# Scores of each head over its own 64 rows, in banks of their own

## Chip, cores and metric

The kernel runs on one core of a Trainium2 chip. The metric is the device time of one execution in microseconds (us). Three timed runs of the kernel before gave 193.37, 194.30 and 194.61; the median is 194.3.

## What is computed

An attention with a narrow window and block summaries, then a feed-forward with a maximum of two projections. Batch is 4, heads 8, sequence 768, head dimension 64:

```
k_sum = k.reshape(B, H, nb, 32, D).max(axis=3)         # nb = 24 blocks of 32 keys
v_sum = v.reshape(B, H, nb, 32, D).mean(axis=3)
scores_l = scale * q @ k.T      where |i - j| < 16, else -1e9
scores_s = scale * q @ k_sum.T + log(32)
a = softmax(concat(scores_l, scores_s))
x = a @ concat(v, v_sum)                               # heads side by side: 3072 x 512
out = maximum(x @ w1, x @ w2) @ w_out                  # 512 -> 1024 -> 512
```

Inputs and the output are float32; the kernel multiplies in bfloat16 and accumulates in float32.

## The kernel before

Each batch is handled in pairs of heads (`hp`, 4 of them). The two heads of a pair lie on the two halves of the 128 partitions, 64 rows of head dimension each.

- `load_kq` (L270) loads k and q of a pair; `prep` casts them to bfloat16 (L340), turns them on TensorE (PE) with 6 transposes each (L359), and places k in a tile `kx` on VectorE (DVE, L373), where each of 12 tiles has 64 keys and, beside them, the 24 block maxima (L375, L382). ScalarE (ACT) places q in `qx` (L388). `qx` has two copies of the sequence, one for each head: head 0's q stands in rows 0 to 63 of the first, head 1's in rows 64 to 127 of the second, and the other halves are zero (`zero_qx`, L216 and L217, once per buffer). So one matmul over all 128 rows gives the scores of both heads side by side.
- `scores` works on a group (`grp`, 3 per pair) of 4 tiles of 64 queries: 4 matmuls of 128 columns (L414; in the last group one is split into 96 and 32). In batch 0 the window's mask is added by two matmuls of 256 columns from `hide` (L403); in the others DVE multiplies with `mask` afterwards (L435, L441). One exp on ACT (L426) reads the group's whole bank of 512 columns into `pb`.
- `values` multiplies `pb` with the values and means in `vx` (L460, 8 matmuls of 65 columns); DVE divides by the sums (L472, L474); two pairs are turned (L484) into `xt` (L489).
- `load_v` loads v (L281), casts it on GpSimd (POOL) into `vb` (L340), spreads it by DMA into `vx` (L304), makes means on PE (L313), and spreads these too (L327).
- `maxout` per batch and group: 32 matmuls of 256 columns with w2 - w1 (`wd`, L560), relu on ACT (L565), then the output: 8 matmuls with w1 @ w_out (`w1o`, L574) and 16 with w_out (L581), copied by ACT (L340) and stored by the SP queue (L592, L594). `w1o` is made in the kernel from w1, turned (L516), and w_out (L544).

The order of all this on each engine isn't written by hand. Every step is a task with an engine, a cost in us and a priority; `Plan.run` (L97) plays the tasks through with these costs and takes, per engine, the first ready one; the resulting start order is the program's order. Buffers come from rings (`Ring`, `Buf`): a slot counts as free 0.15 us after its last user's planned end. The 8 banks of PSUM are one ring with caps by kind (two for scores, "sc"). The waits in the built program come from the data that instructions touch, not from the plan.

Of the kernel before, what the change touches and what calls it, by code (L numbers as in the profile page):

```python
# [62 lines left out]
class Plan:  # L63
# [8 lines left out]
    def op(self, engine, us, fn, read=(), write=(), change=(), touch=(), behind=(), prio=0.0, label=""):  # L72
        t = Task()
        t.engine, t.us, t.fn, t.label = engine, us, fn, label
        t.prio = (prio, len(self.tasks))
        t.new, t.behind = [*write, *change], behind
        t.deps = {w for b in (*read, *change) for w in b.writers}
        for b in t.new:
            b.writers.append(t)
        for b in (*read, *touch, *t.new):  # L80
            b.users.append(t)
        self.tasks.append(t)
        return t
# [45 lines left out]
def kernel(  # L129
# [31 lines left out]
    def tiles(name, n, shape, dt):  # L161
        return [const.tile(shape, dt, name=f"{name}{i}") for i in range(n)]


    banks = Ring(list(range(8)), {"kq": 2, "sc": 2, "av": 2, "mm": 3})
    bank_tile = psum.tile([128, 8, 512], F32, name="banks")

    def bank(buf, n=512, dt=F32):
        a = bank_tile[:, buf.slot]
        return (a if dt is F32 else a.bitcast(BF16))[:, 0:n]  # L170

    kqf = Ring(tiles("kqf", 6, [128, 2, J * D], F32))
    kqb = Ring(tiles("kqb", 4, [128, J, 2, D], BF16))
    kxr = Ring(tiles("kx", 4, [128, KW], BF16))
    qxr = Ring(tiles("qx", 4, [128, 2, S], BF16))
    pbr = Ring(tiles("pb", 12, [128, 4, 192], BF16))
    vfr = Ring(tiles("vf", 2, [128, 4, NM, D], F32))
    vbr = Ring(tiles("vb", 1, [128, NM, H, VW], BF16))
# [30 lines left out]
    def fixed_parts():  # L209
        def once(ring, i, us, fn, prio):  # L210
            b = Buf(ring)
            b.take(i)
            op("DVE", us, fn, write=[b], prio=prio, label=f"zeros {i}")

        def zero_qx(t):
            nc.vector.memset(t[0:64, 1], 0.0)  # L216
            nc.vector.memset(t[64:128, 0], 0.0)  # L217

        def zero_kx(t):
            sums = t[:, 0:96 * NT].rearrange("p (t c) -> p t c", c=96)  # L220
            nc.vector.memset(sums[:, :, 64 + nb:96], 0.0)

        for i, t in enumerate(kxr.slots):
            once(kxr, i, 0.15, lambda t=t: zero_kx(t), i - 1)
        for i, t in enumerate(qxr.slots):
            once(qxr, i, 0.9, lambda t=t: zero_qx(t), i - 1)
        for i, t in enumerate(pbr.slots):
            once(pbr, i, 0.2, lambda t=t: nc.vector.memset(t[:, :, 64:128], 0.0), i / 3 - 1)

        def keep(m, base, row, pattern):  # L230
            nc.gpsimd.affine_select(out=m, in_=m, compare_op=ALU.is_ge, fill=NEG, base=base,
                                    channel_multiplier=row, pattern=pattern)

        def make_hide():

            nc.gpsimd.memset(hide[:], 0.0)
            for lo, hi, base in ((0, 64, -16), (96, 128, 96 - 48)):
                keep(hide[lo:hi], base + window - 1, 1, [[0, 4], [-1, 64]])  # L240
                keep(hide[lo:hi], window - 1 - base, -1, [[0, 4], [1, 64]])
            keep(hide[64:96], nb - 1, -1, [[0, 4], [0, 64]])
            nc.gpsimd.memset(hide[0:64, 3, 48:64], NEG)
            nc.gpsimd.memset(hide[96:128, 3, 0:48], NEG)

        def make_amean():

            nc.gpsimd.memset(amean[:], 0.0)
            am = amean[:, :, 64:64 + nb]
            nc.gpsimd.memset(am, 1.0 / block)  # L250
            for base, mult, pat in ((0, 1, [[128, NM], [-block, nb]]),
                                    (block - 1, -1, [[-128, NM], [block, nb]])):
                nc.gpsimd.affine_select(out=am, in_=am, compare_op=ALU.is_ge, fill=0.0, base=base,
                                        channel_multiplier=mult, pattern=pat)
            for t in vbr.slots:
                nc.gpsimd.memset(t[:, :, :, D:VW], 1.0)

        op("POOL", 4.0, make_hide, write=[hide_in], prio=-1, label="hide")
        op("POOL", 2.0, make_amean, write=[amean_in], prio=0.2, label="amean")
        op("POOL", 0.4, lambda: nc.gpsimd.tensor_scalar(  # L260
            out=mask[:], in0=hide[:], scalar1=-1.0 / NEG, scalar2=1.0, op0=ALU.mult, op1=ALU.add),
           read=[hide_in], write=[mask_in], prio=100, label="mask")
# [81 lines left out]
    def prep(b, hp, prio, k_on, q_on):  # L344
# [21 lines left out]
        def order(ps):  # L366
            return bank(ps, S, BF16).rearrange("p (j c) -> p c j", j=J)

        def kt():
# [13 lines left out]
            out=kt()[:, :, 64:64 + nb],  # L383
            in_=ks.ap[:].rearrange("p (o n) -> p o n", o=1).to_broadcast([128, NT, nb])),
           read=[ks], write=[kx[b, hp]], prio=prio, label=f"sums k{tag}")
        for a in range(2):
            r = slice(64 * a, 64 * a + 64)
            op("ACT", 0.8, lambda a=a, r=r: nc.scalar.copy(  # L388
                out=qx[b, hp].ap[r, a, :], in_=order(qps)[r]),
               read=[qps], write=[qx[b, hp]], prio=prio, label=f"place q{tag}")  # L390

    def scores(b, hp, grp, prio, mask_on):


        ps, pb, tag = Buf(banks, "sc"), Buf(pbr), f"{b}{hp}{grp}"

        def view():
            return bank(ps).rearrange("p (i a w q) -> p i a w q", i=2, a=2, w=2)

        def mm():  # L400
            if mask_on == "PE":
                for i in range(2):
                    nc.tensor.matmul(  # L403
                        out=view()[:, i], lhsT=identity[:],
                        rhs=(hide[:, 2 * i:2 * i + 2] if grp == NG - 1 else hide[:, 0:2]).rearrange(
                            "p (o w) q -> p o w q", o=1).to_broadcast([128, 2, 2, 64]),
                        start=(i == 0), stop=False)
            for i in range(4):
                t = 4 * grp + i
                w = kx[b, hp].ap[:, 96 * t:96 * t + 128]  # L410
                at, o = 64 * t + 16, view()[:, i // 2, :, i % 2]
                for n0, n1 in ((0, 64),) if t < NT - 1 else ((0, 48), (48, 64)):
                    c = (at + n0) % S
                    nc.tensor.matmul(out=o[:, :, n0:n1], lhsT=w,  # L414
                                     rhs=qx[b, hp].ap[:, :, c:c + n1 - n0],
                                     start=(mask_on != "PE"),
                                     stop=(mask_on != "PE" or (i == 3 and n1 == 64)))

        op("PE", 0.25 + (0.23 if mask_on == "PE" else 0), mm, read=[kx[b, hp], qx[b, hp], hide_in],
           write=[ps], prio=prio, label=f"scores {tag}")  # L420

        def pv():
            a = pb.ap[:, :, 0:128]
            return bass.AP(a.tensor, a.offset, [a.ap[0], a.ap[1], [128, 2], [1, 64]])

        op("ACT", 0.7, lambda: nc.scalar.activation(  # L426
            out=pv(), in_=bank(ps).rearrange("p (i w q) -> p i w q", w=2, q=64),
            func=ACT.Exp, bias=bias[:], scale=scale),
           read=[ps], write=[pb], prio=prio, label=f"exp {tag}")

        def hidden_out():
            eng = nc.vector if mask_on == "DVE" else nc.gpsimd
            if grp < NG - 1:
                m = mask[:, 0:1].rearrange("p w (o q) -> p w o q", o=1).to_broadcast([128, 4, 2, 64])
                eng.tensor_tensor(out=pv(), in0=pv(), in1=m, op=ALU.mult)  # L435
            else:
                o = pv().rearrange("p (i a) w q -> p i a w q", a=2)
                for i in range(2):
                    m = mask[:, 2 * i:2 * i + 2].rearrange("p (o w) q -> p o w q", o=1).to_broadcast(
                        [128, 2, 2, 64])  # L440
                    eng.tensor_tensor(out=o[:, i], in0=o[:, i], in1=m, op=ALU.mult)  # L441

        if mask_on != "PE":
            op(mask_on, 0.43 if grp < NG - 1 else 0.56, hidden_out, read=[mask_in], change=[pb], prio=prio,
               label=f"mask {tag}")
        return pb
# [3 lines left out]
    def values(b, hp, grp, pb, prio):  # L450
# [5 lines left out]
        def mm():  # L456
            for u in range(2):
                for a in range(2):
                    for par in range(2):
                        nc.tensor.matmul(out=av()[:, u, a, :],  # L460
                                         lhsT=pb.ap[:, 2 * u + a, 64 * par:64 * par + 128],
                                         rhs=vx[b].ap[:, 4 * grp + 2 * u + par, 2 * hp + a, 0:D + 1],
                                         start=(par == 0), stop=(par == 1))

# [211 lines left out]
```

## Time and profile before

| | |
|---|---|
| median of three runs | 194.3 us |
| the profiled execution, first to last instruction | 192.5 us |
| PE busy | 166.4 us (86%) |
| ACT busy | 114.1 us (59%) |
| DVE busy | 109.9 us (57%) |
| mean granted PE clock | 0.991 |
| score matmuls (L414) | 208 |
| exps (L426) | 48, 0.686 us each |
| placing q (L388) | 32, 0.791 us each |

The profiled execution has no time beside its span; the timed runs lie 0.9 to 2.1 us above it. Busy times are from one execution. PE's loads of weights (PEld) run beside its matmuls, and a matmul's recorded duration is longer than the distance to the next one, so the distance between starts is the better price of a matmul. A group's line gives: source line, engine, operation, output and input tiles, shapes and count; then busy us and mean ns; then the engine's idle time before, and who ended it. A line of waits gives: who waited for whom, us in total, times, longest.

### The profile page before, as it was taken

How to read it: one execution, taken by the hardware profiler on the slowest of the kernel's cores; microseconds unless marked ns; L12 is line 12 of the kernel's file. 1: busy time of each engine (PE TensorE's matmuls, PEld its weight loads, DVE VectorE, ACT ScalarE, POOL GpSimd, SP SyncE). 2: the span in 40 equal slices, each digit the busy share in tenths (PEclk: the TensorE clock that was granted, in tenths of full speed). 3: DMA queues.
4: the chain of work that ended last, by engine and by line, in shares of the span. 5: the costliest groups of instructions: out<-in, count | busy, mean ns of one | idle time of the engine just before them, and what ended most of it. 6: DMA issues, size and time to landing. Idle time of an engine off the chain costs nothing.

```text
span 192.5 us, 4148 instructions
## 1 busy us (share of the span) xinstructions
PE 166.4 (86%) x1643; PEld 117.9 (61%) x1664; DVE 109.9 (57%) x289; ACT 114.1 (59%) x173; POOL 25.7 (13%) x39
## 2 busy tenths in 40 slices
PE   0629619899999969999979999999999999999990
PEld 0426419865757738758657767487696676665740
DVE  6908956888979438759868953079777600000000
ACT  2533964384689949219967955179986443342621
POOL 7556221300330003300003300000000000000000
PEclk9999996999999999999999999999999999999999
DMA  5999999999999999999999996061020111120303
GB/s 187 226 305 356 234 240 347 371 381 281 210 359 251 292 268 217 339 309 217 229 288 223 340 218 193 3 164 24 3 109 5 54 58 59 50 109 0 112 0 109
DMA packets 47859, 37.27 MB, mean 194 GB/s; under 512 B 26208, under 2 KB 43744, under 8 KB 47840
## 3 DMA queue, kind: packets, MB, share of 16 engines
q1 hardware_dynamic: 47840, 37.01, 71.8%
q8 instruction: 13, 0.21, 0.5%
q14 instruction: 6, 0.05, 0.1%
HBM read 25.17 MB, written 6.29 MB: 163 GB/s over the span
## 4 chain that ended last, share of the span: by engine, by line
PE 53%; DMA 33%; SPq 5%; DVE 4%; POOL 2%; issue 1%; ACT 0%; ACTq 0%
PE banks L581 17%; PE banks L560 16%; DMA vf<-in_v_dram 13%; DMA vx<-vb 10%; PE banks L574 7%; PE banks L460 5%; DMA wf<-in_moe_w_out_dram 4%; SPq L503 4%; DMA vx<-vx 4%; PE banks L414 3%; DMA kqf<-in_k_dram 2%; PE banks L359 2%; POOL vb L340 2%; PE banks L484 2%; PE banks L313 1%; DVE pb L435 1%
## 5 line engine op out<-in xcount | busy, mean ns | idle before, releaser
L560 PE MATMUL banks<-xt,wd 128*128 128x256 bf16 x384 | 46.6, 273 | 0.5 <-DVE xt L489 0.5
L581 PE MATMUL banks<-wo,g 128*128 128x512 bf16 x184 | 44.9, 379 | 0.4
L560 PEld LDWEIGHTS <-wd 128*128 128x128 bf16 x384 | 36.4, 98 | 6.1 <-issue 0.7
L426 ACT ACTIVATE pb<-banks,bias 128x512 bf16<-128x512 f32 x48 | 31.5, 686 | 10.2 <-PE banks L414 9.9
L565 ACT ACTIVATE g<-banks 128x512 bf16<-128x512 f32 x48 | 28.3, 596 | 13.7 <-PE banks L560 13.2
L340 ACT COPY o<-banks 128x512 f32<-128x512 f32 x24 | 14.0, 585 | 28.7 <-PE banks L581 28.4
L388 ACT COPY qx<-banks 64x768 bf16<-64x768 bf16 x32 | 25.3, 791 | 6.1 <-PE banks L359 5.8
L581 PEld LDWEIGHTS <-g 128*128 128x128 bf16 x192 | 17.2, 97 | 16.5
L460 PE MATMUL banks<-vx,pb 128*128 128x65 bf16 x384 | 19.4, 196 | 3.6 <-DMA vx<-vx 1.8
L574 PE MATMUL banks<-w1o,xt 128*128 128x512 bf16 x85 | 21.9, 379 | 0.6
L460 PEld LDWEIGHTS <-pb 128*128 128x128 bf16 x384 | 16.9, 100 | 7.1 <-DMA vx<-vx 2.1
L359 PE MATMUL banks<-identity,kqb 128*128 128x128 bf16 x192 | 16.6, 234 | 5.3 <-DVE kqb L340 4.7
L340 ACT CAST kqb<-kqf 128x768 bf16<-128x768 f32 x16 | 13.1, 830 | 13.6 <-DMA kqf<-in_q_dram 8.7
L414 PE MATMUL banks<-qx,kx 128*128 128x128 bf16 (+2 forms) x208 | 18.6, 226 | 2.3 <-ACT qx L388 1.3
L340 POOL CAST vb<-vf 128x1536 bf16<-128x1536 f32 x8 | 12.2, 1520 | 55.0 <-DMA vf<-in_v_dram 35.2
L474 DVE TENSOR_TENSOR xs<-banks,inv 128x256 bf16<-128x256 f32 x48 | 19.1, 415 | 0.3
L414 PEld LDWEIGHTS <-kx 128*128 128x128 bf16 x208 | 15.1, 103 | 6.6 <-DVE kx L382 2.4
L359 PEld LDWEIGHTS <-kqb 128*128 128x128 bf16 x192 | 13.6, 106 | 8.5 <-DVE kqb L340 4.7
L373 DVE COPY kx<-banks 128x768 bf16<-128x768 bf16 x16 | 15.2, 955 | 2.9 <-PE banks L359 1.7
L375 DVE TENSOR_REDUCE ks<-kx 128x24 bf16<-128x768 bf16 x16 | 15.1, 944 | 0.1
L489 DVE COPY xt<-banks 128x512 bf16<-128x512 bf16 x24 | 9.8, 418 | 7.2 <-PE banks L484 6.8
L574 PEld LDWEIGHTS <-xt 128*128 128x128 bf16 x96 | 8.9, 98 | 7.9
(47 smaller groups left out, 129.8 us busy)
## 6 DMA issues: line engine op xcount, KB each, us to landing
kqf<-in_k_dram SPq DMA_DIRECT2D x16, 384.0 KB, 6.6
kqf<-in_q_dram SPq DMA_DIRECT2D x16, 384.0 KB, 5.7
vf<-in_v_dram SPq DMA_DIRECT2D x8, 768.0 KB, 10.7
out_dram<-o SPq DMA_DIRECT2D x20, 256.0 KB, 2.2
wf<-in_moe_w_dram SPq DMA_DIRECT2D x8, 512.0 KB, 11.1
vx<-vb SPq DMA_DIRECT2D x6, 396.0 KB, 8.0
wf<-in_moe_w_out_dram SPq DMA_DIRECT2D x4, 512.0 KB, 8.6
vx<-vx SPq DMA_DIRECT2D x4, 363.0 KB, 6.2
```

The lines of the kernel that those rows point to most:

```text
L340: {"DVE": nc.vector.tensor_copy, "ACT": nc.scalar.copy, "POOL": nc.gpsimd.tensor_copy}[engine](out=o, in_=i)
L359: nc.tensor.transpose(out=bank(ps, S, BF16)[:, 128 * j:128 * j + 128], in_=src.ap[:, j].rearrange("p h d -> p (h d)"), identity=identity[:])
L373: op("DVE", 0.96, lambda: nc.vector.tensor_copy(out=kt()[:, :, 0:64], in_=order(kps)), read=[kps], write=[kx[b, hp], kmain], prio=prio, la ...
L388: op("ACT", 0.8, lambda a=a, r=r: nc.scalar.copy(out=qx[b, hp].ap[r, a, :], in_=order(qps)[r]), read=[qps], write=[qx[b, hp]], prio=prio, ...
L414: nc.tensor.matmul(out=o[:, :, n0:n1], lhsT=w, rhs=qx[b, hp].ap[:, :, c:c + n1 - n0], start=(mask_on != "PE"), stop=(mask_on != "PE" or (i ...
L426: op("ACT", 0.7, lambda: nc.scalar.activation(out=pv(), in_=bank(ps).rearrange("p (i w q) -> p i w q", w=2, q=64), func=ACT.Exp, bias=bias ...
L460: nc.tensor.matmul(out=av()[:, u, a, :], lhsT=pb.ap[:, 2 * u + a, 64 * par:64 * par + 128], rhs=vx[b].ap[:, 4 * grp + 2 * u + par, 2 * hp ...
L474: op("DVE", 0.42, lambda: nc.vector.tensor_tensor(out=x.ap[:, hp % 2], in0=av()[:, :, :, 0:D], in1=inv.ap[:].to_broadcast([128, 2, 2, D]), ...
L560: nc.tensor.matmul(out=bank(ps)[:, 256 * s:256 * s + 256], lhsT=wd[n].ap[:, c, 128 * s:128 * s + 128], rhs=x.ap[:, c, :], start=(c == 0), ...
L565: op("ACT", 0.6, lambda n=n, ps=ps: nc.scalar.activation(out=g.ap[:, 2 * n:2 * n + 2, :].rearrange("p f n -> p (f n)"), in_=bank(ps), func ...
L574: nc.tensor.matmul(out=bank(ps), lhsT=x.ap[:, c, sl], rhs=w1o[c].ap[:], start=(c == 0), stop=False)
L581: nc.tensor.matmul(out=bank(ps), lhsT=g.ap[:, f, sl], rhs=wo[f // 2].ap[:, f % 2, :], start=False, stop=(f == FC - 1))
```

## The change

`qx` loses its second copy: q is placed with one copy over 128 rows, and nothing is zeroed. Each score matmul now takes one head's 64 rows of `kx` and of `qx` and writes 64 columns; head 0's scores go to PSUM bank 0, head 1's to bank 1. A group holds 256 columns of each of these two banks; two groups share them (`halves`, columns 0 and 256). The ring of the other uses has the remaining 6 banks. The mask of batch 0 is added by one matmul per head and bank. The exp reads both banks, and `pb` now has head before tile pair (`2 * a + u` instead of `2 * u + a`), which the mask and the values follow. No cost in the plan's tasks is changed, but one place-q task is left of two, and the zeroing tasks are gone.

```
-    banks = Ring(list(range(8)), {"kq": 2, "sc": 2, "av": 2, "mm": 3})
+    banks = Ring(list(range(2, 8)), {"kq": 2, "av": 2, "mm": 3})
+    halves = Ring([0, 256])
...
-        a = bank_tile[:, buf.slot]
+        a = bank_tile[:, buf.ap]
...
-    qxr = Ring(tiles("qx", 4, [128, 2, S], BF16))
+    qxr = Ring(tiles("qx", 4, [128, S], BF16))
...
-        def zero_qx(t):
-            nc.vector.memset(t[0:64, 1], 0.0)
-            nc.vector.memset(t[64:128, 0], 0.0)
...
-        for i, t in enumerate(qxr.slots):
-            once(qxr, i, 0.9, lambda t=t: zero_qx(t), i - 1)
...
-        for a in range(2):
-            r = slice(64 * a, 64 * a + 64)
-            op("ACT", 0.8, lambda a=a, r=r: nc.scalar.copy(
-                out=qx[b, hp].ap[r, a, :], in_=order(qps)[r]),
-               read=[qps], write=[qx[b, hp]], prio=prio, label=f"place q{tag}")
+        op("ACT", 0.8, lambda: nc.scalar.copy(out=qx[b, hp].ap[:], in_=order(qps)),
+           read=[qps], write=[qx[b, hp]], prio=prio, label=f"place q{tag}")
...
-        ps, pb, tag = Buf(banks, "sc"), Buf(pbr), f"{b}{hp}{grp}"
+        ps, pb, tag = Buf(halves), Buf(pbr), f"{b}{hp}{grp}"
...
+        def view(a):
+            return bank_tile[:, a, ps.ap:ps.ap + 256]
 
         def mm():
             if mask_on == "PE":
-                for i in range(2):
+                for a in range(2):
                     nc.tensor.matmul(
-                        out=view()[:, i], lhsT=identity[:],
...
-                        start=(i == 0), stop=False)
+                        out=view(a), lhsT=identity[:],
+                        rhs=hide[:] if grp == NG - 1 else hide[:, 0:1].to_broadcast([128, 4, 64]),
+                        start=True, stop=False)
             for i in range(4):
                 t = 4 * grp + i
...
                 for n0, n1 in ((0, 64),) if t < NT - 1 else ((0, 48), (48, 64)):
                     c = (at + n0) % S
-                    nc.tensor.matmul(out=o[:, :, n0:n1], lhsT=w,
-                                     rhs=qx[b, hp].ap[:, :, c:c + n1 - n0],
...
+                    for a in range(2):
+                        r = slice(64 * a, 64 * a + 64)
+                        nc.tensor.matmul(out=view(a)[:, 64 * i + n0:64 * i + n1],
+                                         lhsT=kx[b, hp].ap[r, 96 * t:96 * t + 128],
+                                         rhs=qx[b, hp].ap[r, c:c + n1 - n0],
+                                         start=(mask_on != "PE"),
+                                         stop=(mask_on != "PE" or (i == 3 and n1 == 64)))
...
         op("ACT", 0.7, lambda: nc.scalar.activation(
-            out=pv(), in_=bank(ps).rearrange("p (i w q) -> p i w q", w=2, q=64),
+            out=pv(), in_=bank_tile[:, 0:2, ps.ap:ps.ap + 256].rearrange("p a (u w q) -> p a u w q", u=2, w=2),
             func=ACT.Exp, bias=bias[:], scale=scale),
...
-                                         lhsT=pb.ap[:, 2 * u + a, 64 * par:64 * par + 128],
+                                         lhsT=pb.ap[:, 2 * a + u, 64 * par:64 * par + 128],
```

More of the change, by code (lines that the diff above doesn't have):

```diff
@@ L392, in scores @@
     def scores(b, hp, grp, prio, mask_on):
-        ps, pb, tag = Buf(banks, "sc"), Buf(pbr), f"{b}{hp}{grp}"
-        def view():
-            return bank(ps).rearrange("p (i a w q) -> p i a w q", i=2, a=2, w=2)
+        ps, pb, tag = Buf(halves), Buf(pbr), f"{b}{hp}{grp}"
+        def view(a):
+            return bank_tile[:, a, ps.ap:ps.ap + 256]
         def mm():
             if mask_on == "PE":
-                for i in range(2):
+                for a in range(2):
                     nc.tensor.matmul(
-                        out=view()[:, i], lhsT=identity[:],
-                        rhs=(hide[:, 2 * i:2 * i + 2] if grp == NG - 1 else hide[:, 0:2]).rearrange(
-                            "p (o w) q -> p o w q", o=1).to_broadcast([128, 2, 2, 64]),
-                        start=(i == 0), stop=False)
+                        out=view(a), lhsT=identity[:],
+                        rhs=hide[:] if grp == NG - 1 else hide[:, 0:1].to_broadcast([128, 4, 64]),
+                        start=True, stop=False)
@@ L408, in mm @@
             for i in range(4):
                 t = 4 * grp + i
-                w = kx[b, hp].ap[:, 96 * t:96 * t + 128]
-                at, o = 64 * t + 16, view()[:, i // 2, :, i % 2]
+                at = 64 * t + 16
                 for n0, n1 in ((0, 64),) if t < NT - 1 else ((0, 48), (48, 64)):
                     c = (at + n0) % S
-                    nc.tensor.matmul(out=o[:, :, n0:n1], lhsT=w,
-                                     rhs=qx[b, hp].ap[:, :, c:c + n1 - n0],
-                                     start=(mask_on != "PE"),
-                                     stop=(mask_on != "PE" or (i == 3 and n1 == 64)))
+                    for a in range(2):
[5 more added lines that the diff above has]
+                                         stop=(mask_on != "PE" or (i == 3 and n1 == 64)))
@@ L436, in hidden_out @@
             else:
-                o = pv().rearrange("p (i a) w q -> p i a w q", a=2)
-                for i in range(2):
-                    m = mask[:, 2 * i:2 * i + 2].rearrange("p (o w) q -> p o w q", o=1).to_broadcast(
+                o = pv().rearrange("p (a u) w q -> p a u w q", a=2)
+                for u in range(2):
+                    m = mask[:, 2 * u:2 * u + 2].rearrange("p (o w) q -> p o w q", o=1).to_broadcast(
                         [128, 2, 2, 64])
-                    eng.tensor_tensor(out=o[:, i], in0=o[:, i], in1=m, op=ALU.mult)
+                    eng.tensor_tensor(out=o[:, :, u], in0=o[:, :, u], in1=m, op=ALU.mult)
         if mask_on != "PE":
```

## The prediction

> **What bounds the kernel now.** I read the table of engines and the slices first, then three stretches of the span, then who waited for whom, then groups and single pieces of the timeline.
>
> ```profile
> PE 166.4 (86%) x1643; PEld 117.9 (61%) x1664; DVE 109.9 (57%) x289; ACT 114.1 (59%) x173; POOL 25.7 (13%) x39
> ...
> PE   0629619899999969999979999999999999999990
> ...
> DMA  5999999999999999999999996061020111120303
> ```
>
> For some 34 us (seven slices of 4.8 us) PE has holes and DMA is full: the start waits for loads. From there PE is full to the end; ACT and DVE are not.
>
> ```profile
> 34.30:70.42 36.12, 32.91 (x325) 22.55 (x330) 28.05 (x64) 26.19 (x38) 4.36 (x5) 1.00 1.09 304
> 70.42:97.36 26.94, 25.43 (x292) 18.85 (x297) 20.08 (x54) 16.58 (x26) 3.05 (x3) 1.00 1.06 266
> 97.36:192.50 95.14, 89.56 (x844) 62.13 (x855) 38.86 (x113) 53.50 (x86) 3.17 (x2) 1.00 0.38 103
> ```
>
> After a stretch's bounds and length come the busy times of PE, PEld, DVE, ACT and POOL, the granted clock (1.00) and DMA. Two of the bounds are places where PE last waited for a transfer:
>
> ```profile
> PE banks L460 <- DMA vx<-vx: 1.8, 1, 1.8
> PE banks L460 <- DMA kqf<-in_k_dram: 1.3, 1, 1.3
> PE banks L414 <- ACT qx L388: 1.3, 1, 1.3
> PE banks L544 <- ACT wo L340: 0.4, 1, 0.4
> ```
>
> The first ends at 70.42 (batch 1's values, gate 1), the second at 97.36 (batch 2's, gate 2), the last at 41.0 (w_out). The one wait for a placed q lies at 8.6 us, ahead of a wait for v that lasts to 14.2. PE never waits for an exp (L426). So from 41 us on the time is PE's own work and whatever stops PE.
>
> **Prices.**
>
> ```profile
> L426 ACT ACTIVATE pb<-banks,bias 128x512 bf16<-128x512 f32 x48 | 31.5, 686 | 10.2 <-PE banks L414 9.9
> L388 ACT COPY qx<-banks 64x768 bf16<-64x768 bf16 x32 | 25.3, 791 | 6.1 <-PE banks L359 5.8
> L414 PEld LDWEIGHTS <-kx 128*128 128x128 bf16 x208 | 15.1, 103 | 6.6 <-DVE kx L382 2.4
> ```
> ```profile
> 57.10 0.61 PE L414 MATMUL banks<-qx,kx 128*128 128x128 bf16 x8
> 57.53 1.26 ACT L426 ACTIVATE pb<-banks,bias 128x512 bf16<-128x512 f32 x2 [0.48 <-PE banks L414]
> ...
> 71.98 0.41 PE L460 MATMUL banks<-vx,pb 128*128 128x65 bf16 x8
> 72.22 0.39 PE L414 MATMUL banks<-qx,kx 128*128 128x128 bf16 x4
> 72.44 0.41 PE L460 MATMUL banks<-vx,pb 128*128 128x65 bf16 x8
> ```
>
> A step's price on PE is the distance between starts: 8 matmuls of 65 columns take 72.22 - 71.98 = 0.24 us, 30 ns each; 4 of 128 take 0.22, 56 each. In the same way 256 columns cost 109 and 512 cost 216. The second line shows that two exps behind each other take 1.26 us and start about 0.03 us after their last matmul's end.
>
> **The change, part by part.**
>
> *Placing q once, no zeroing.* 16 copies of 128x768 in place of 32 of 64x768: I take 0.79 us each, as a 128x768 cast on ACT (L340, 0.83) is hardly dearer than the 64x768 copy, so ACT loses 12.7 us; bounds 0.79 and 1.58 (then nothing is saved). DVE loses 8 memsets of 0.38, 3.0 us. Neither is on the path: the only wait that it shortens (1.3 us at 8.6) is followed by the wait for v. Worth 0, at most 0.5.
>
> *Score matmuls.* 416 of 64 rows x 64 columns in place of 208 of 128 x 128 (and 96, 32). By L460's row at 30 ns they are 12.5 us against 11.0: +1.5 in all. Bounds: 15 ns each if the two heads' halves truly run side by side (-4.7 us over batches 1 to 3), 56 if each costs what one of 128 columns does (+8).
>
> *Shared banks, the new wait.* All scores now go through banks 0 and 1: group A writes columns 0 to 255 of both, group B 256 to 511. In the built program's order the semaphores treat a bank as one thing: an exp waits for the last score matmul written to its bank, also the other half's, and a score group waits for the exp before it in ACT's order, whichever half that read. PE is in order, so behind the waiting scores stand values (L460), maxout (L560, L581) and transposes (L359); ACT and DVE wait for those in turn. With two exps between, scores can go on 0.03 + 0.16 (the tail of a 0.19 matmul) + 1.26 + 0.05 = 1.5 us after the pair; with one exp, 0.9. I put PE's work that stands between against this, priced as above. Batch 1: two groups short by 0.3 each before gate 1. Behind gate 1 eight groups are short, by 0.39, 0.1, 0.64, 0.64, 0.63, 0.33, 0.17 and 0.64: 3.5 us, all behind gate 2. The others (1.1 to 2.2 us of work between) are covered. In batch 0 five groups wait too (up to 1.5 each), but there PE waits for w1 anyway (4.0 us before 28.6); without that cover they'd cost 6.
>
> *The order.* The planner sees ACT tasks gone and other banks, and moves things. Batch 0's 12 score groups now all stand ahead of its first values, behind two w1 transposes more. At the wait for w_out (41.0) 146.0 us of PE's work is still to come against 142.0; at gate 1 120.3 against 115.2 (8 of L574, 8 of L560, 8 of L581 less are done, 4.3 us, and dearer scores 0.8); at gate 2 92.2 against 89.8. On SP, two stores (L592) now stand behind batch 1's last spread (L327) where they stood ahead of it, so gate 1 may open up to 1.8 us earlier.
>
> *Change of rows.* PE goes into 64-row matmuls and back 39 times, 27 of them in batches 1 to 3; the trace has no half-height matmul. Least: nothing, as between 128x128 and 128x65 above. Most: PE runs empty (219 - 56 = 163 ns for L414) and then loads weights uncovered (98, L414's median): 0.26 each way. I take the load alone, 0.10, since loads lie beside matmuls everywhere here (PEld 117.9 us beside PE) and the first across the change is what can't.
>
> *Sum.* From 41.0: 146.0 - 120.3 = 25.7 of work, 1.0 of small gaps as before, 0.6 of exp waits, 10 row changes 1.0: gate 1 at 69.3, about when the spread lands. Then 28.2 with gaps, 8 changes 0.8: gate 2 reached at 98.3, later than it opens. Then 92.2, gaps 0.9, exp waits 3.5, 26 changes (8 of 34 find PE stopped) 2.5: PE ends at 197.4, against 188.1. That is +9.3: span 201.8. The runs shown have a median 1.8 us above the span; I add 9.3 to 194.3 and get 203.6.
>
> **The rivals.**
>
> 1. *Full emptying at each change of rows*, 0.26 each way: gate 1 at 70.9, gate 2 at 101.3, end 204.3, +16.3: 210.6 us. For it: every weight load would have to wait for matmuls that use all rows. Against: nothing seen in this trace, where changes of form are free. The Trainium skill speaks for it: TensorEngine Tiling (Array Packing), section Key Properties, says that a change of tiling mode, not of tile alone, drains the engine. It gives no price; no run here shows it yet.
>
> 2. *Only the waits and the order*, row changes free: 194.1, +6.0: 200.3; with halves running side by side less 3.5 to 4.7, near 196.
>
> 3. *Faster: both heads' halves in the array at once.* Place: the 36 score groups of batches 1 to 3, each 0.13 instead of 0.23 us, -3.4 us against before, with row changes free. It decides if the exp waits and the lost head start stay under 3.4, which needs the eight waits to vanish (ACT idle enough to start each exp at once; the order then costs the 2.5 us left at gate 2, less 1.3 of idle there): 194.3 - 3.4 + 1.2, near 192. Against it: the waits stand in the program, and 1.26 us of exps doesn't fit under 0.86 of work. The Trainium skill, TensorE: Matmul & The Clock Gate, section The mechanism in Part 3, has tiles of different rows start about 4 ns apart; by that the pair is nearly one matmul.
>
> 4. *The change doesn't do what it says*: the halves queue one behind the other and 64-row loads don't lie under matmuls: 56 ns and row changes too, +9.3 + 8: 211.
>
> **How the numbers follow.** The forecast (waits, order, some cost per row change; 201 to 207) 0.42; rival 1 and 4 together 0.25; rival 2 0.24, of which 0.05 ends within 1%; rival 3 0.05, of which 0.04 is faster; 0.04 for something milder, within 1%. A difference of 1% (about 2 us) is what a measurement here can tell from none. So faster 0.04, same 0.10, slower 0.86. Range: from rival 2 with halves side by side (197) to rivals 1 and 4 (211).
>
> **What would show it.** Right: waits of PE's scores for ACT's pb of some 4 us in all, in batches 2 and 3 most; score matmuls about 30 ns apart; PE's last matmul at 195 to 199 us; ACT's place q 16 x 0.8. Row changes show as a gap of 0.1 to 0.26 us ahead of the first score matmul of a run and of the first matmul behind it. Wrong: no such waits (then the order or the pairs decide), starts in pairs (rival 3), or gate 1 or 2 opening later than 70.4 and 97.4 because the loads' order has changed, which I count as nothing.

## The result, and the profile after

The changed kernel took 201.76 us (median of four runs, 200.12 to 202.54); the kernel before, on the same chip, 194.46. The ratio is 1.043 with an interval of 1.036 to 1.050: slower by 4%. The forecast was 203.6, with a range of 197 to 211. The profiled execution after took 202.54 us, with a span of 200.8. Here and below, medians and ranges count every run, while ratios and their intervals leave out the runs that took over 1.5% longer than the fastest one of the same kernel.

The engines and slices of the page after:

```profile
PE 171.3 (85%) x1851; PEld 115.3 (57%) x1872; DVE 106.5 (53%) x281; ACT 101.2 (50%) x157; POOL 25.3 (13%) x39
...
PE   0538775789999899999588959999899999999991
...
PEclk9999955599999999999999999999999999999999
DMA  5999999999999999999999991133110110211203
```

ACT lost 12.9 us of work and the end came 8.3 us later: ACT was not the bound. PE's row has two new holes, the 5 in slice 20 (gate 2) and the one in slice 24 (a wait for an exp, at 117 to 119 us), and PE's granted clock is at half in slices 6 to 8 (from 26.1 to 39.7 us in the trace).

The same three stretches, between the new places of the gates (69.11 and 99.50):

```profile
34.30:69.11 34.81, 31.32 (x369) 21.49 (x372) 28.71 (x70) 21.26 (x31) 4.19 (x5) 0.92 1.09 297
69.11:99.50 30.39, 27.99 (x334) 20.10 (x339) 18.02 (x53) 15.22 (x25) 3.05 (x3) 1.00 1.11 258
99.50:200.80 101.30, 92.63 (x943) 61.84 (x954) 40.43 (x116) 49.61 (x81) 2.94 (x2) 1.00 0.34 98
```

Gate 1 is not later (69.1, before 70.4). The second stretch is 3.5 us longer and the last one 6.2: that is where the time went. What PE waited for behind 41 us:

```profile
PE banks L406 <- ACT pb L419: 3.2, 4, 2.0
PE banks L453 <- DMA vx<-vx: 2.6, 2, 2.0
```

The first line, score matmuls waiting for exps, was not there before. The second is the two gates, 0.6 at gate 1 and 2.0 at gate 2, where the waits were 1.8 and 1.3 before. The groups:

```profile
L419 ACT ACTIVATE pb<-banks,bias 128x512 bf16<-128x512 f32 x48 | 31.2, 684 | 17.9 <-PE banks L406 17.8
...
L406 PEld LDWEIGHTS <-kx 64*128 64x128 bf16 x416 | 9.6, 99 | 14.3 <-issue 11.9
...
L381 ACT COPY qx<-banks 128x768 bf16<-128x768 bf16 x16 | 12.5, 802 | 8.0 <-PE banks L354 7.9
```

An exp and a copy cost what they cost before (684 and 802 ns against 686 and 791), the copy for twice the rows. A 64-row weight load costs as much as one of 128 rows (99 ns, before 103). And one piece of the timeline after, with the start of each step in the first column:

```profile
71.89 0.41 PE L406 MATMUL banks<-qx,kx 64*128 64x64 bf16 x16
72.23 1.04 PE L574 MATMUL banks<-wo,g 128*128 128x512 bf16 x4
```

From the first of 16 half-height matmuls to the next step's start is 0.34 us. 16 at the forecast's 30 ns would be 0.48 with no gap at all. The single starts of this run in the trace, in ns:

```
values (128 rows)   71703 71732 71765
scores (64 rows)    71889 71892   71928 71931   71957 71960   71986 71990
                    72015 72019   72045 72048   72074 72077   72103 72106
output (128 rows)   72229
```

Three things are to be read here. The starts come in pairs, the two heads 3 ns apart, and one pair follows the other after 29 ns: 14.5 ns each. From the last matmul of 65 columns to the first score it is 124 ns, 94 more than such a matmul takes. From the last score to the output it is 123 ns, 108 more than its 14.5.

**The books behind w_out.** Each kernel's PE from the first matmul of w1o on: its start, the work that the program still holds, priced by distance between starts (512 columns 216 ns, 256 109, 128 56, 65 30, two half-height ones 29), what is left over as time not worked (waits, gaps, and what stretches at half the clock cost), and the last matmul's start, all in us.

| kernel | w1o starts | work left | not worked | last start |
|---|---|---|---|---|
| before | 40.6 | 141.8 | 5.2 | 187.6 |
| after | 42.3 | 141.1 | 13.0 | 196.4 |
| heads in turn | 41.3 | 141.1 | 10.6 | 193.1 |
| all rows | 42.9 | 145.6 | 6.3 | 194.7 |
| plan as before | 40.5 | 138.2 | 10.6 | 189.3 |
| plan knows banks | 41.8 | 141.1 | 7.4 | 190.3 |
| same rows (scores at 29) | 42.1 | 145.6 | 8.7 | 196.4 |
| shared, 4 other banks | 41.9 | 141.1 | 17.1 | 200.1 |
| both mends of the plan | 42.2 | 137.3 | 9.5 | 189.0 |

The last start moved by 8.8: 1.6 from a later start, -0.7 of work, 7.8 of time not worked. The 13.0 are 27 runs of half-height matmuls at 0.2 (entry 93 to 96 ns, exit 84 to 108 ns, by size of the last matmul): 5.4; exp waits of 3.9 (the sum over all runs of what their entry takes beyond 95 ns; the page's 3.2 leaves short ones out); the gates' 2.6; and 1.1 of small gaps. In two rows the time not worked also holds 3.4 us at half the clock, just behind gate 1: from 70.5 to 73.9 with 4 other banks, from 71.5 to 75.0 with both mends.

### The profile page after: what moved, and what is told of

Its sections match the earlier page's. It is cut to its first block, busy times and chain, and to the rows that moved or that the text cites. A ratio compares the mean times of both kernels' runs of the same rounds, so it can differ in the third digit from the quotient of the medians.

```text
span 200.8 us, 4530 instructions
## 1 busy us (share of the span) xinstructions
PE 171.3 (85%) x1851; PEld 115.3 (57%) x1872; DVE 106.5 (53%) x281; ACT 101.2 (50%) x157; POOL 25.3 (13%) x39
## 4 chain that ended last, share of the span: by engine, by line
PE 53%; DMA 25%; SPq 7%; DVE 7%; ACT 2%; issue 2%; POOL 1%; ACTq 0%
PE banks L574 17%; PE banks L553 15%; DMA vx<-vx 8%; PE banks L567 8%; DMA wf<-in_moe_w_out_dram 5%; DMA vf<-in_v_dram 5%; SPq L276 4%; PE banks L453 4%; DMA kqf<-in_q_dram 3%; DMA kqf<-in_k_dram 3%; PE banks L308 3%; PE banks L354 2%; PE banks L406 2%; PE banks L477 2%; DVE ks L370 2%
## 5 line engine op out<-in xcount | busy, mean ns | idle before, releaser
L553 PE MATMUL banks<-xt,wd 128*128 128x256 bf16 x384 | 47.5, 273 | 0.2 <-DVE xt L482 0.2
L574 PE MATMUL banks<-wo,g 128*128 128x512 bf16 x186 | 45.6, 379 | 0.6 <-issue 0.5
L419 ACT ACTIVATE pb<-banks,bias 128x512 bf16<-128x512 f32 x48 | 31.2, 684 | 17.9 <-PE banks L406 17.8
L453 PE MATMUL banks<-vx,pb 128*128 128x65 bf16 x384 | 18.9, 198 | 4.7 <-DMA vx<-vx 2.6
L406 PEld LDWEIGHTS <-kx 64*128 64x128 bf16 x416 | 9.6, 99 | 14.3 <-issue 11.9
L406 PE MATMUL banks<-qx,kx 64*128 64x64 bf16 (+2 forms) x416 | 13.3, 196 | 3.9 <-ACT pb L419 3.2
L381 ACT COPY qx<-banks 128x768 bf16<-128x768 bf16 x16 | 12.5, 802 | 8.0 <-PE banks L354 7.9
L428 DVE TENSOR_TENSOR pb<-pb,mask 128x512 bf16<-128x512 bf16 x24 | 11.9, 510 | 6.6 <-ACT pb L419 6.6
```

The costliest lines, as they stand in the source:

```text
L406: nc.tensor.matmul(out=view(a)[:, 64 * i + n0:64 * i + n1], lhsT=kx[b, hp].ap[r, 96 * t:96 * t + 128], rhs=qx[b, hp].ap[r, c:c + n1 - n0], ...
L419: op("ACT", 0.7, lambda: nc.scalar.activation(out=pv(), in_=bank_tile[:, 0:2, ps.ap:ps.ap + 256].rearrange("p a (u w q) -> p a u w q", u=2 ...
L453: nc.tensor.matmul(out=av()[:, u, a, :], lhsT=pb.ap[:, 2 * a + u, 64 * par:64 * par + 128], rhs=vx[b].ap[:, 4 * grp + 2 * u + par, 2 * hp ...
L553: nc.tensor.matmul(out=bank(ps)[:, 256 * s:256 * s + 256], lhsT=wd[n].ap[:, c, 128 * s:128 * s + 128], rhs=x.ap[:, c, :], start=(c == 0), ...
L574: nc.tensor.matmul(out=bank(ps), lhsT=g.ap[:, f, sl], rhs=wo[f // 2].ap[:, f % 2, :], start=False, stop=(f == FC - 1))
```

## The experiments

All ran three rounds or more against the kernel before, whose medians were 193.92, 193.5 and 194.3 us in the three groups of runs (the first four experiments, the next four, the last two).

**1. Heads in turn.** Are the pairs side by side because the program alternates the heads?

```
-            for i in range(4):
...
-                    for a in range(2):
-                        r = slice(64 * a, 64 * a + 64)
+            for a in range(2):
+                r = slice(64 * a, 64 * a + 64)
+                for i in range(4):
...
```

> The changed kernel with the two heads' score matmuls of a group in turn (all of head 0, then all of head 1) instead of alternating; the order of steps and all waits stay. Theory (halves run side by side: pairs 29 ns apart in the changed kernel, and this pays back about as much as the row changes cost): starts 29 ns apart for each single matmul, so 312 matmuls of batches 1 to 3 x 14.5 ns = +4.5 us, some 206 us against 201.8. Rival (time goes by the planner's order and the transfers' gates alone, PE work is covered): within 1 us of 201.8.

Measured: 200.74 us (199.25 to 201.26), ratio 1.035 (1.028 to 1.042). The cost of 4.5 us did not come. The starts of one run say why:

```
54393 54407 54432 54445 54462 54474 54491 54503
54520 54532 54549 54567 54578 54597 54607 54626
```

They are 15.5 ns apart on average, mostly by turns 10 to 14 and 17 to 19, so 16 take hardly longer than in pairs: four matmuls of one head in turn did not keep the other head's out. The last group of a pair shows how. There each head has five matmuls, of 64, 64, 64, 48 and 16 columns, so the columns tell a matmul's place. All 16 such runs of this trace start them in the same order:

```
as written:  64 64 64 48 16   64 64 64 48 16
as started:  64 64 64 64 64 48 64 16 48 16
```

The first matmul of 48 columns has three of 64 ahead of it in the program and five in the trace, so two of head 1's started ahead of it: PE started matmuls out of the program's order. (In the changed kernel and in experiment 5 they start as written.) The order within a group is not what the low price hangs on, and this run alone could not tell what it hangs on. It did not make the kernel slower either; its time not worked is 2.4 us less (exp waits 2.5 in place of 3.9, as the longest, 2.1 us, is 0.47 here; gate waits 1.7 in place of 2.6).

**2. All rows.** The same banks, exps and order, each matmul over 128 rows (it sums both heads, so the values differ):

```
-  lhsT=kx[b, hp].ap[r, 96 * t:96 * t + 128], rhs=qx[b, hp].ap[r, c:c + n1 - n0],
+  lhsT=kx[b, hp].ap[:, 96 * t:96 * t + 128], rhs=qx[b, hp].ap[:, c:c + n1 - n0],
```

> The changed kernel with each score matmul over all 128 rows (it computes the sum of both heads' products for each, so the scores are not the reference's); same number of matmuls, same 64 columns, same banks, same order and waits. Theory (each step into 64-row matmuls and out costs 0.1 us, 0.2 a run, 27 runs behind 41 us; side by side saves 14.5 ns x 312): 5.4 saved, 4.5 lost, so 200 to 202 us, the gap of 95 ns ahead of a run and of 85 to 108 behind it gone, starts 29 ns apart, waits for exps as before (about 4 us). Rival (the gaps are no row changes but belong to the waits or the loads of kx): the gaps stay, and the time rises by 4.5 to 206.

Measured: 200.69 (200.42 to 203.44), ratio 1.036 (1.029 to 1.043). Starts are 29 ns apart (55.831, 55.859, 55.889, ...), the first 109 ns after the last matmul of 256 columns and the first matmul of 512 columns 29 ns behind the last: no gap at either end. So the gaps belong to the change of row height. Work rose by 4.5 and time not worked fell by 6.7: the row changes' 5.4 are gone and most of the gates' 2.6. The exp waits stayed, and are longer (3.9 us on the page, 3.2 in the changed kernel):

```profile
PE banks L406 <- ACT pb L419: 3.9, 8, 1.7
PE banks L453 <- DVE pb L428: 0.4, 1, 0.4
```

In this kernel, then, what the pairs save (4.5) and what row changes take (5.4) nearly cancel.

**3. Plan as before.** The planner keeps counting the tasks that were taken out, with nothing issued for them:

```
+        for i, t in enumerate(qxr.slots):
+            once(qxr, i, 0.9, lambda: None, i - 1)
...
+        op("ACT", 0.8, lambda: None, read=[qps], write=[qx[b, hp]], prio=prio, label=f"none q{tag}")
```

> The changed kernel, but the planner still counts the removed tasks (a second place q of 0.8 us on ACT per pair, zeroing on DVE), which emit nothing; so the order is close to that of before. Work of PE still to come at the wait for w_out falls from 141.2 to 138.3 us and at batch 1's values from 116.7 to 112.4 (with pairs at 29 ns); scores short of cover behind 41 us by 1.3 instead of 3.8 us. Theory (order and exp waits are what made it slower): 2.5 less wait and 2 to 4 less left at the gates, so 196 to 198 us, still above 194.4 because of some 5 us of row changes less 3.5 of side by side. Rival (the order costs nothing, only row changes and banks do): 199 to 200 us, the waits' part alone.

Measured: 195.82 (194.64 to 200.23, ten runs), ratio 1.011 (1.006 to 1.016): 6 us of the 7.3 gone, by tasks that do nothing. w1o starts at 40.5, as before, and the work left is 138.2: before's 141.8 less the 3.7 that the cheaper scores make (8.2 us for 36 groups before, 312 x 14.5 ns now). In the planner's order (neither half had a run of its own) it is the ACT task that decides: counting it alone gives this same order, counting the zeroing alone gives that of the changed kernel. The order is not that of the kernel before in every step, since the banks differ. It also has few exp waits left:

```profile
PE banks L456 <- DMA vx<-vx: 2.7, 2, 1.7
PE banks L356 <- DVE kqb L337: 1.0, 1, 1.0
PE banks L409 <- ACT pb L422: 0.8, 2, 0.4
```

So order and waits are not two separate costs: the order sets how much work lies between two score groups.

**4. Plan knows the banks.** The order stays free, but no score group is planned while an exp runs:

```
+        if t.label.startswith("scores") and any(
+                e.start is not None and e.done + self.LAG["ACT"] > now for e in self.exps):
+            return False
```

> The changed kernel, but the planner doesn't start a score group while an exp runs; so it knows that both halves lie in the same banks and puts other work of PE between. Nothing else is changed; work left at the gates stays 141.2 and 116.7. Theory (the shared banks stop PE 3.9 us behind 41 us): waits of scores for exps behind 41 us near 0 by the order (all covered by 1.4 us of work or more), and 197 to 199 us. Rival (PE would only wait elsewhere, for values, masks or transfers, as the stall is given back at gate 2): waits gone but time within 1 us of 201.8.

Measured: 197.21 (196.49 to 198.9), ratio 1.020 (1.012 to 1.027). Work left is 141.1 as in the changed kernel; time not worked fell from 13.0 to 7.4. The waits behind 41 us:

```profile
PE banks L410 <- DVE kx L381: 0.5, 1, 0.5
PE banks L457 <- DMA vx<-vx: 0.4, 1, 0.4
PE banks L557 <- DVE xt L486: 0.2, 1, 0.2
```

No line of scores waiting for an exp is left, and 5.4 of the 7.4 are the row changes. By the medians the gain is 4.5 us. Between the two profiled executions the last start moved by 6.1: 3.9 of waits for exps, 2.2 of the gates' 2.6 and 0.5 of the start, less the new wait for `kx` of 0.5. So 3.9 can't be read off the gain alone.

**5. Same rows.** Both heads' matmuls on rows 0 to 63 (head 1's scores are then head 0's), so that nothing can lie side by side:

```
-                        r = slice(64 * a, 64 * a + 64)
+                        r = slice(0, 64)
```

> The changed kernel with both heads' score matmuls over rows 0 to 63 (so the second head gets the first head's scores); number, size, banks, order and waits stay, row changes stay, but no two of them use different rows. Taking the heads in turn did not separate them: their starts still came two in 29 ns. Theory (two halves side by side save 14.5 ns each): starts 29 ns apart, +4.5 us behind 41 us, 205 to 206 us against 201.8. Rival (a 64-row matmul of 64 columns is short by itself, whichever rows it uses): starts still some 15 ns apart and no change beyond 1 us.

Measured: 202.48 (201.64 to 202.91), ratio 1.046 (1.039 to 1.053). The starts are now 29 ns apart, singly:

```
55193 55232 55262 55291 55320 55349 55378 55407 ...
```

So half-height matmuls on the same rows cost 29 ns and only different rows make it 14.5: this settles what experiment 1 could not. By the time alone the rival (no change) would seem to hold: work rose by 4.5, but the total by only 0.7 against the changed kernel. The time not worked fell by 4.3 beside it. The waits for exps fell from 3.9 to 2.4, and all of that at one place: the longest, 2.1 us in the changed kernel, is 0.45 here, and the others kept their size. At gate 1 PE stood 0.8 us, and at gate 2 not at all:

```profile
PE banks L406 <- ACT pb L419: 1.5, 4, 0.4
PE banks L453 <- DMA vx<-vx: 0.8, 1, 0.8
```

**6 and 7. Other banks for the second group.** A control with four banks for other uses, and the same order with group B in banks 2 and 3 instead of the other halves of 0 and 1 (the first edit is in both, the second, and the exp with it, in experiment 7 alone):

```
-    banks = Ring(list(range(2, 8)), {"kq": 2, "av": 2, "mm": 3})
+    banks = Ring(list(range(4, 8)), {"kq": 2, "av": 2, "mm": 3})
...
-            return bank_tile[:, a, ps.ap:ps.ap + 256]
+            return bank_tile[:, a + ps.ap // 128, 0:256]
```

> The changed kernel with 4 instead of 6 banks for everything but the scores (banks 2 and 3 stay unused), scores in the halves of banks 0 and 1 as before it. It is the control for the next: order of steps the same there. By the order scores are short of cover by 2.4 us behind 41 us and by 5 before. Theory: some 201 to 203 us, waits for exps about 2.4 us behind 41 us. Rival (fewer banks for the others hold PE up by themselves): over 204.

> As the control with 4 other banks, with the very same order of steps, but the second score group lies in banks 2 and 3 of its own. Theory (it is the shared bank that makes scores wait for the exp of the other group and exps for the other group's scores): waits for exps behind 41 us 0 by the order, so 2.4 us less there than the control and up to 3 less before 41, where loads cover part: 197 to 200 us, 2 to 4 below the control. Rival (PE would have stopped elsewhere): within 1 us of the control.

Measured: the control 206.45 (206.29 to 208.81), ratio 1.070 (1.061 to 1.079); apart 206.15 (202.18 to 208.27), ratio 1.053 (1.039 to 1.066). Control, then apart, waits behind 41 us:

```profile
PE banks L453 <- DMA vx<-vx: 2.9, 1, 2.9
PE banks L453 <- ACT g L558: 1.5, 2, 1.0
PE banks L406 <- ACT pb L419: 1.2, 3, 0.4
PE banks L477 <- DVE xs L467: 0.7, 2, 0.5
```
```profile
PE banks L453 <- ACT g L558: 2.6, 2, 2.1
PE banks L453 <- DMA vx<-vx: 2.6, 1, 2.6
PE banks L453 <- DMA vx<-vb: 1.5, 1, 1.5
```

The control missed its expectation, and its rival (over 204) came: with four banks PE waits for ACT's relu to empty one (1.5 us, not there before) and stands 2.9 us at gate 1 (0.6 in the changed kernel), and the whole is 4.7 us above the changed kernel. In experiment 7 the control's line of scores waiting for an exp (L406, 1.2 us) is gone, so the wait does come from sharing a bank, as forecast. The 2 to 4 us below the control that were expected of it are not shown: the medians are 0.3 apart, the intervals of the two ratios overlap, and what the sharing is worth in time stays open here.

**8. Both mends of the plan**, experiments 3 and 4 together:

> The changed kernel with both mends of the planner: it still counts the removed tasks, and starts no score group while an exp runs. Work left at w_out is 137.5 us, at batch 1's values 113.3; no score group short of cover behind 41 us, where the plan as before alone had 1.3. Theory: 1 to 1.5 us below the plan as before alone (195.8), so 194 to 195 us, about what the kernel before takes, with 25 runs x 0.2 us of row changes against 3.8 of side by side left. Rival (what is left above before is not the waits): 195.5 or more.

Measured: 194.3 (193.7 to 199.12, ten runs), ratio 1.003 (0.998 to 1.008): level with before. The pairs, the row changes and the shared banks are all still in it. What the changed kernel lost is thus the order of its plan, and the waits that this order ran into.

**9. Groups by twos.** If a run costs 0.2 us, fewer runs should beat both kernels. On top of experiment 8, batches 1 to 3 have two groups in one PE step (and their values' tasks are made behind all of the batch's scores, with the priorities that they had):

```
+            op("PE", 0.5, lambda: (mm0(), mm()), read=[kx[b0, hp0], qx[b0, hp0], kx[b, hp], qx[b, hp]],
+               write=[ps0, ps], prio=prio0, label=f"scores {tag0} {tag}")
```

> Both mends of the plan stay (the removed ACT task is still counted, no scores are planned under a running exp), and in batches 1 to 3 two groups of scores are one step, so that 18 runs of half-height matmuls stand behind w_out's matmuls in place of 25; 137.6 us of PE work behind them as there. Theory (each run costs about 0.2 us, in and out): 7 x 0.2 = 1.4 us less than the version with both mends alone, 192.5 to 193.5. Rival (what a row change costs is hidden by waits that come anyway, or two exps behind each other hold the next scores longer): no change, 194 to 195. It would be above 195 if the steps of two groups delay the values and gates open later.

> The version with both mends of the plan once more, on the chip of the version with two groups in a step, as its control: 194 to 195, level with before.

Measured: 194.07 (192.95 to 197.69, 13 runs), ratio 1.001 (0.997 to 1.006); the control 193.6 (192.85 to 195.72), ratio 1.000 (0.997 to 1.004). The 1.4 us did not come: the rival holds. Waits for transfers behind 41 us, two groups in a step, then control:

```profile
PE banks L473 <- DMA vx<-vx: 3.8, 2, 3.6
PE banks L473 <- DMA vx<-vb: 1.7, 1, 1.7
```
```profile
PE banks L460 <- DMA vx<-vx: 2.8, 2, 2.2
PE banks L581 <- issue: 0.2, 1, 0.2
```

With two groups in a step PE waited 5.5 us for spread values, the control 2.8. A faster PE reaches its gates earlier, and the gates open when the spreads land. This is a hint only: the trace with two groups in a step is of an execution of 197.69 us, 3.6 over the median, while the control's took 194.18. In that trace PE also had half the granted clock from 97.7 to 104.5 us, and it worked from 99.1 on; an estimate from these figures is 2.7 us lost, which is most of the 3.6. The control's trace has no such stretch between 35.2 us and its last matmul. No version beat the kernel before.

## Why the prediction was right, and where it was not

The direction, the range and the main mechanism held: waits for exps, the order of the plan and row changes made the kernel slower. But two of the signs that the prediction named as showing it wrong came as well, starts in pairs and a gate 2 that opened later than 97.4. The price of a score matmul was off by -4.8 us, and start, gates and row changes together by +5.0. That these cancelled is luck, and that the forecast came within 1.8 us rests on it.

- *Shared banks' waits.* Forecast 0.6 + 3.5 = 4.1 us; measured 3.9. Experiments 4 and 7 remove them in two ways. But the single waits were not the forecast ones: one of 2.1 makes more than half. It shows how a wait is handed on:

```profile
116.45 0.83 ACT L335 CAST kqb<-kqf 128x768 bf16<-128x768 f32 x1 [2.91 <-DMA kqf<-in_q_dram]
...
117.19 0.59 ACT L558 ACTIVATE g<-banks 128x512 bf16<-128x512 f32 x1
117.68 1.26 ACT L419 ACTIVATE pb<-banks,bias 128x512 bf16<-128x512 f32 x2
...
118.99 0.30 PE L406 MATMUL banks<-qx,kx 64*128 64x64 bf16 x10 [2.03 <-ACT pb L419]
```

  ACT stood until 116.45 for q of a later pair, so relu and two exps came late, and PE's scores behind the second exp with them. The forecast put ACT's exps at once behind their matmuls. In experiments 1 and 5 ACT doesn't stand there and the same wait is 0.47 and 0.45, so some 1.6 of the 3.9 us hang on that late q. The Trainium skill says, PSUM — Partial Sum Buffer, section PSUM bank collisions raise a hardware error, that PSUM is to be guarded by bank (or by bank and quadrant) and not by address; the built program does so, as experiment 7 shows, and the 3.9 us, with the late q in them, are what that costs here.
- *Score matmuls.* Forecast 30 ns each and +1.5 us; measured 14.5, the lower bound of the text: the pairs of rival 3 are there. This is the step that failed, by 4.8 us over 312 matmuls (146.0 of work left became 141.1). The sentence on the Trainium skill, TensorE: Matmul & The Clock Gate, section The mechanism in Part 3, holds: starts 3 ns apart against its 4 or so. The row of 65 columns over all rows, from which I took 30, was right for half-height matmuls on the same rows (29, experiment 5) and not for different ones.
- *Change of rows.* Forecast 0.10 each way; measured 0.093 to 0.096 in and 0.084 to 0.108 out. The bound 0.26, a PE run empty and then a load, fell, and rival 1 with it. Trainium skill, TensorEngine Tiling (Array Packing), section Key Properties: that a change of mode drains the engine agrees in that there is a gap, which experiment 2 shows to belong to the rows alone; its size is well under 0.26. In all it made 5.4 in place of 4.3, since runs at which PE was stopped paid as well.
- *Gate 1.* Forecast 69.3, measured 69.1; but PE had come some 0.6 us earlier and stood for the spread, which set the time. *Gate 2:* forecast reached at 98.3 with no wait. PE stood 2.0 us there until 99.5. The spread was issued 1.7 us earlier than before (90.24, before 91.95) and took 9.2 us to land, before 5.4. The queue after, and then before:

```profile
90.24 0.62 SPq L322 DMA_DIRECT2D vx<-vx  x1
90.91 0.61 SPq L276 DMA_DIRECT2D vf<-in_v_dram  x1
92.83 7.07 SPq L585 DMA_DIRECT2D out_dram<-o  x1
```
```profile
91.95 0.61 SPq L327 DMA_DIRECT2D vx<-vx  x1
93.01 0.40 SPq L270 DMA_DIRECT2D kqf<-in_k_dram  x1
93.82 1.05 SPq L270 DMA_DIRECT2D kqf<-in_q_dram  x1
94.91 4.98 SPq L281 DMA_DIRECT2D vf<-in_v_dram  x2
```

  The loads' order counted as nothing in the forecast, and the text named that as a way to be wrong. After, a load of v is issued 0.7 us behind the spread; before, one of k came 1.1 us and those of v 3.0 us behind it. Whether that made the spread slow was not tried and stays open.
- *The start.* w1o began at 42.3, forecast 41.0. The clock granted in 36.0 to 40.6 was 0.60, before 1.00, and eight matmuls of 65 columns took 0.46 us from 37.99 on, 0.24 at the full clock. Batch 0's waits for exps were costed at nothing, since PE would wait for weights anyway. What the text left out is the clock: in the changed kernel it was at half from 26.1 to 39.7 us, before from 29.3 to 32.7. From 28 to 36 us PE was busy for 4.7 of the 8 us, before for 7.2; that this standing kept the clock down is a guess from these figures and not shown. Nor does the clock alone settle the start: with the plan as before (half until 31.2) w1o started at 40.5, with both mends (half until 34.0) at 42.2.
- *Placing q and zeroing.* Forecast: 12.7 us less on ACT and 3.0 on DVE, worth 0. ACT fell by 12.9 and DVE by 3.4; nothing was gained. That the freed 12.7 us of ACT would reorder the plan and so cost, was in the forecast as an effect, +4.0 of work left behind w_out (1.2 of it dearer scores, by the forecast's own prices; the order's part measured 2.9, 141.1 against 138.2 in experiment 3). How much of the loss hung on it was not: experiment 3 gives 6 us of 7.3.
- *From span to time.* The last start came at 196.4 where PE was to end at 197.4: the pairs' -4.8 were met by +1.3 of start, +2.6 of gates and +1.1 of row changes, with -0.9 of small gaps and -0.2 of exp waits. The other 0.8 of the miss of 1.8 us is the spread of the runs: all runs here took 1.6 to 2.0 us more than their spans, and the one that was profiled, 202.54 us, was the slowest of its four, 0.8 over the median.
- *Rival 3's second half*, that the waits vanish, is what experiment 8 made true, and still it was level and not faster: the 3.7 us that the scores are cheaper than before stand against some 5.0 for 25 runs' row changes.

## What to carry to other kernels

Half-height matmuls for two heads nearly halve the time of the score matmuls themselves (8.2 to 4.5 us), but every run of them costs about 0.2 us at its ends; count runs as well as matmuls, and expect no gain where a run is 8 or 16 matmuls of 64 columns long, as here. Where a planner sets the order, taking a task out is also a change of the order, and it can cost more than the task: try the new code under the old plan first. And if two users come to share a bank, tell the planner, since the built program guards banks and not columns.

## What the runs showed of the hardware that I had not expected

Half-height matmuls on different rows overlap even when four of one head stand ahead of four of the other: 15.5 ns apart on average in experiment 1, against 14.5 in pairs and 29 on the same rows. PE started some of the other head's ahead of their place in the program: in all 16 runs of that trace with matmuls of 48 columns, the first of these started behind five of 64 columns, where the program has three ahead of it. A weight load of 64 rows takes as long as one of 128 (99 ns against 103). The gap ahead of a run does not depend on what ran before (94 ns behind 65 columns, 96 behind 256 and 512), while the gap behind it is 108 ns when the last score matmul had 64 columns and 84 to 86 when it had 16.
